# Linear attention into a Swish feed-forward: attention of batch 1 in fewer bursts, another order of loads, later relus

## The chip, the cores and the metric

The kernel runs on one core of a Trainium2 chip. The metric is the device time of one execution in microseconds (us). The core's engines each have a queue of their own and work in the order in which the program issues to them: TensorE (PE; PEld is its load of weights), VectorE (DVE), ScalarE (ACT), GpSimd (POOL) and SyncE (SP), which issues most DMAs.

## The reference, cut to what matters

```python
# q, k, v: (8, 8, 576, 64): batch, head, position, width
phi(x) = concat(relu(x) * cos, relu(x) * sin)     # cos, sin depend on the position
kv  = einsum('bhsf,bhsd->bhfd', phi(k), v);  z = sum_s phi(k)
x   = (phi(q) @ kv) / (phi(q) @ z + 1e-6)         # per batch and head
x   = x.transpose(0, 2, 1, 3).reshape(4608, 512)
h   = x @ w_in                                    # 512 -> 2048
out = (h * sigmoid(beta * h)) @ w_out             # 2048 -> 512
```

## The kernel before, in words

The 4608 tokens are worked through in nine chunks of 512 (eight blocks of 64 tokens). A batch has nine blocks, so chunk 0 holds blocks 0 to 7 of batch 0, chunk 1 block 8 of batch 0 and blocks 0 to 6 of batch 1, chunk 2 blocks 7 and 8 of batch 1 and six of batch 2, and so on. The program is a hand-written order (`manual_schedule`): each engine's queue holds its instructions in the order of the code, and the framework adds the waits that the data need.

**Attention of a batch.** `load_raw` brings queries, keys and values in from SP (L79). `q_relu`, `k_relu` (L192 on ScalarE, L193 on VectorE) and `v_scale` (L217 ScalarE, L219 VectorE) make qb, rk and vb in bf16. The queries are turned, by TensorE (`q_turn_pe`, L235, with copies qt on ScalarE, L240, and products with the tangent, qs, on VectorE, L223) or by a DMA (`q_turn_dma`, L259). `kv_mm` (L276) makes kv of a pair of heads from 36 products on 64x64 tiles, `kv_take` copies it out of PSUM (L286). `num_mm` (L297) makes eight products on 64x64 tiles for one block and one half jp of the heads. `x_rden` and `x_mul` (L308, L312, L319) divide, and xs is turned into xt by TensorE (`x_turn_pe`, L356, copies L361 and L363) or by a DMA from SP (`x_turn_dma`, L367).

**Feed-forward.** `h_mm` (L386) multiplies xt by w_in, for four slices mi of which the first two need the half jp 0 of the heads and the others jp 1; `h_act` (L394) is the Swish on ScalarE. In chunk 0 the second product is plain (`o_mm`, L544, copy L550). For chunk 1 (`o_fast`, L563) and the later ones it is done with sums of blocks (S1 to S4 from the Swish's results, T1 to T4 from w_out, L406 and L876 to L879 on VectorE), seven products "1" to "7" for each pair of token groups; the copies "c1", "cu", "c5", "c4" (L602, L604, L603, L582) and the sums "a2", "a3", "a7" (L606, L607, L608) move partial results between them.

**Chunk 0** has 32 slots. Slots 0 to 15 are the sixteen groups of `h_mm` and `h_act`, slots 16 to 31 the second product, four matmuls of 128x512 for each group and weight slice; slot 24 + i needs slice 8 + i of w_out, which `cast_out` (L121 ScalarE, L123 VectorE) scales into bf16. The table `early` hangs other work behind a slot. Before the change it holds: slot 4, the two `num_mm` of block 8 of batch 0 and `rest()` (casts of w_in, loads of w_out and of batch 1, block 8's `x_mul` and its turn by DMA, casts of w_out, values, keys and queries of batch 1); slot 15, parts of values and keys on ScalarE; slot 22, both `kv_mm` of batch 1; slot 23, `second()`, the turn of its queries; slots 25 and 26, seven blocks of `num_mm` for each half; slots 28 and 29, the turns of xs. At slot 24 the loads of batch 2 are issued.

**Chunk 1** has sixteen slots of `h_group`. Behind slot 0 come blocks 7 and 8 of batch 1 (`num_rest`) and the queries of batch 2, at slots 2 to 5 its values and keys, at slot 6 the sums T, at slot 10 `kv_all(2)` and the tangent. Behind the slots ScalarE makes the relus of batch 3's queries, and only then do the products "1" and their copies "c1" follow.

PSUM has eight banks; the banks that a product takes are named in the code (block 8 took banks 2 and 3, each half of sevens 4 and 5 or 6 and 7, the rest 2 and 3).

Of the kernel before, what the change touches and what calls it, by code (L numbers as in the profile page):

```python
# [22 lines left out]
def kernel(  # L23
# [52 lines left out]
    def load_raw(b, name, j0=0, j1=4):  # L76
        js = slice(j0, j1)
        src = {"q": q, "k": k, "v": v}[name][b]
        nc.sync.dma_start(  # L79
            out=raw_tile(b, name)[:, js].rearrange("q j n d -> q j (n d)"),  # L80
            in_=src.rearrange("(j g) (p n) d -> (g p) j (n d)", g=2, n=NQ)[:, js, :])
# [46 lines left out]
    load_raw(0, "q", 0, 2)  # L128
    load_raw(0, "q", 2, 4)
    beta16 = const.tile([JT, P], FP32, name="beta16")  # L130
    nc.scalar.dma_start(out=beta16, in_=moe_beta.rearrange("(j p) -> j p", p=P))
    load_raw(0, "v", 0, 2)
    load_raw(0, "k", 0, 2)
# [115 lines left out]
    def qs_of(b):  # L249
        return wx["q"] if b > 3 and b % 2 == 0 else qs_first  # L250
# [30 lines left out]
    def kv_take(jps, bank, eng="dve"):  # L281
# [5 lines left out]
        else:  # L287
            nc.vector.tensor_copy(o, a)

    def num_mm(b, n, jp, bank, slot):  # L290

        for cs in range(2):
            for jj in range(2):
                rows = slice(jj * HP, (jj + 1) * HP)
                for g in range(2):
                    cols = slice(g * HP, (g + 1) * HP)
                    nc.tensor.matmul(  # L297
                        ps[cols, bank + jj, slot * E : (slot + 1) * E],
                        lhsT=(qts[b % 2], qs_of(b))[cs][rows, jp, n, cols],
                        rhs=kv[rows, g, jp, cs, :],  # L300
                        start=(cs == 0), stop=(cs == 1))

    def x_rden(bank, slot, n0, n1, jps):

        w, m = len(jps), n1 - n0
        nv = ps[:, bank : bank + 2, slot * E : (slot + w * m) * E].rearrange("q j (i s e) -> q j i s e", s=w, e=E)
        den = small.tile([P, 2, m, w], FP32, name="den", tag=f"den{m}{w}")
        nc.vector.tensor_tensor(  # L308
            den, nv[:, :, :, :, D],
            eps9[:, n0:n1].unsqueeze(1).unsqueeze(3).to_broadcast([P, 2, m, w]), op=ALU.add)  # L310
        rden = small.tile([P, 2, m, w], FP32, name="rden", tag=f"rden{m}{w}")
        nc.vector.reciprocal(rden, den)  # L312
        return nv, rden, n0, jps

    def x_mul(got, n0, n1):
        nv, rden, first, jps = got
        a, z, w = n0 - first, n1 - first, len(jps)
        o = xs[:, n0:n1, jps[0] : jps[-1] + 1].rearrange("q n s (j d) -> q j n s d", j=2)
        nc.vector.tensor_tensor(  # L319
            o.rearrange("q j n s d -> q j (n s) d"),  # L320
            nv[:, :, a:z, :, 0:D].rearrange("q j n s d -> q j (n s) d"),
            rden[:, :, a:z].rearrange("q j n s -> q j (n s)").unsqueeze(3).to_broadcast([P, 2, (z - a) * w, D]),
            op=ALU.mult)
# [432 lines left out]
    def cast_halves(i, fs=(0, 256)):  # L756
        for f in fs:
            for gj in GJ:
                cast_win(i, gj, "pool" if i > 1 and gj == GJ[3] else "dve", f, f + 256)
# [2 lines left out]

    def rest():

        cast_halves(2)
        cast_halves(3)
        x_mul(x_rden(2, 0, 8, NQ, (0, 1)), 8, NQ)
        load_w("out", 0)
        load_w("out", 1)
        load_raw(1, "v")  # L770
        load_raw(1, "k")
        load_raw(1, "q")
        load_w("out", 2, 2)
        load_w("out", 3, 2)
        x_turn_dma(0, 8, 9)
        for j in range(8):
            cast_out(j)
        v_scale(1, 0)
        v_scale(1, 1, n0=8)
        k_relu(1, 0, 2)  # L780
        q_relu(1, 0)
        q_relu(1, 1, n1=5)

# [2 lines left out]
        for n in range(7):  # L786
            num_mm(1, n, jp, bank, n)

    takes = []

    def second():

        takes.append(q_turn_pe(1, 0, 4, hold=True))
        takes.append(q_turn_pe(1, 1, 6, hold=True))
        cast_out(8)
        takes[0]("act", 0)
        takes[0]("dve", 1)
        cast_out(9, "a")
        takes[0]("dve", 0)
        takes[0]("act", 1)  # L800
        cast_out(10)
        for e, i in (("act", 0), ("dve", 1), ("act", 1), ("dve", 0)):
            takes[1](e, i)
        for j in (11, 12, 14, 15):
            cast_out(j, "a")

    early = {
        4: lambda: (num_mm(0, 8, 0, 2, 0), num_mm(0, 8, 1, 2, 1), rest()),
        15: lambda: (v_scale(1, 1, n1=8, eng="act"), k_relu(1, 2, 4, "act")),
        22: lambda: (kv_mm(1, 0, 6), kv_mm(1, 1, 6), kv_take((0, 1), 6, "act"), q_relu(1, 1, "act", 5)),  # L810
        23: second,
        25: lambda: (num_seven(0, 4), x_mul(x_rden(4, 0, 0, 7, (0,)), 0, 7), cast_out(13)),
        26: lambda: (num_seven(1, 6), x_mul(x_rden(6, 0, 0, 7, (1,)), 0, 7)),
        28: lambda: x_turn_pe(1, 0, 7, 4, ("act",), (0,)),
        29: lambda: x_turn_pe(1, 0, 7, 5, ("dve",), (1,)),
    }

    def num_rest():
        for n in range(7, NQ):
            for jp in range(2):  # L820
                num_mm(1, n, jp, 2, 2 * (n - 7) + jp)
        x_mul(x_rden(2, 0, 7, NQ, (0, 1)), 7, NQ)
        x_turn_dma(1, 7, NQ)

# [29 lines left out]
    for slot in range(32):  # L854
        if slot < 4:
            if slot == 0:
                for jt in range(2):
                    h_mm(0, jt, (2, 3), slice(0, 4))
            h_mm(0, slot, (2, 3), slice(4 if slot < 2 else 0, 8))
            h_act(0, slot)  # L860
        elif slot < 16:
            h_group(0, slot)
        elif slot < 24:
            o_part(0, slot % 4, (slot - 16) // 4)
        else:
            for tt in range(4):
                o_mm(0, tt, (slot - 16,))
        if slot == 24:
            for name in "qvk":
                load_raw(2, name)  # L870
        if slot in early:
            early[slot]()

# [5 lines left out]
        nc.vector.tensor_tensor(T3, B22, B12, op=z)  # L879

    wx_tiles()
    for slot in range(16):
        h_group(1, slot)
        if slot == 0:
            num_rest()
            att_q(2)
            v_half(2, 0)
        if 2 <= slot < 6:
            v_half(2, 1, slot + 3, slot + 4, "act")
        if slot == 4:  # L890
            k_all(2)
            v_half(2, 1, 0, 5)
        elif slot == 6:
            w_sums()
        elif slot == 10:
            kv_all(2, eng="act")
            for jp in range(2):
                tan_mul(nc.vector, qs_of(2)[:, jp], qts[0][:, jp], 0, NQ)
    q_relu(3, 0, "act")
    q_relu(3, 1, "act")  # L900
    q_turn_dma(3)

    def one_sums(kind):
        for i0 in range(0, JT // 2, 2):
            g_sum(1, i0, i0 + 2, kind)
# [6 lines left out]
    ops(x, "1 c1")  # L912
    one_sums(1)
    ops(y, "1 c1")
    for t, bank in enumerate((4, 6, 0)):
        num_all(2, t, bank)
    one_sums(2)
# [174 lines left out]
```

## Time and profile before

| what | us |
|---|---|
| median of 3 runs (273.54 to 273.8) | 273.59 |
| the profiled execution | 274.44 |
| its span in the profile | 272.7 |
| PE busy in the span | 265.3 |
| DVE busy | 224.0 |
| ACT busy | 188.4 |
| POOL busy | 68.3 |

The span is what the profile covers of the execution; the rest of the execution's time lies around it. A row of a timeline gives start, length, engine, line, operation, what is written from what, shapes and count; in brackets the idle time before it and who ended it. In the chain of work that ended last, each piece is what the next one waited for, or what stood before it on its engine. Where the page says "L386" it means that line of the kernel.

Chunk 0's second product runs from 31.8 to 50.4 us, chunk 1's first product from 50.4 to 65.9, its second to 80.6.

### The profile page before, as it was taken

How to read it: one execution, taken by the hardware profiler on the slowest of the kernel's cores; microseconds unless marked ns; L12 is line 12 of the kernel's file. 1: busy time of each engine (PE TensorE's matmuls, PEld its weight loads, DVE VectorE, ACT ScalarE, POOL GpSimd, SP SyncE). 2: the span in 40 equal slices, each digit the busy share in tenths (PEclk: the TensorE clock that was granted, in tenths of full speed). 3: DMA queues.
4: the chain of work that ended last, by engine and by line, in shares of the span. 5: the costliest groups of instructions: out<-in, count | busy, mean ns of one | idle time of the engine just before them, and what ended most of it. 6: DMA issues, size and time to landing. Idle time of an engine off the chain costs nothing.

```text
span 272.7 us, 8970 instructions
## 1 busy us (share of the span) xinstructions
PE 265.3 (97%) x3712; PEld 206.8 (76%) x3712; DVE 224.0 (82%) x596; ACT 188.4 (69%) x384; POOL 68.3 (25%) x89
## 2 busy tenths in 40 slices
PE   8899999999899999999999999999999999999994
PEld 8554455455784588888888888888888888888883
DVE  5989969499989889789989997899589768757852
ACT  4778777796419656899489966996696179428920
POOL 1444000510078000660085009300840060000001
PEclk9999999999999999999999999999999999999999
DMA  6999999999969999994589439943600570015005
GB/s 237 374 395 383 392 390 319 379 201 336 284 130 311 240 348 226 240 313 103 147 216 370 92 58 223 332 71 62 181 2 2 61 185 1 2 27 130 0 2 155
DMA packets 50681, 54.00 MB, mean 198 GB/s; under 512 B 31232, under 2 KB 31760, under 8 KB 50640
## 3 DMA queue, kind: packets, MB, share of 16 engines
q1 hardware_dynamic: 47504, 45.55, 59.1%
q0 software_dynamic: 2784, 7.61, 9.6%
q8 instruction: 29, 0.48, 0.7%
q10 hardware_dynamic: 352, 0.27, 0.4%
q14 instruction: 12, 0.10, 0.1%
HBM read 36.71 MB, written 9.44 MB: 169 GB/s over the span
## 4 chain that ended last, share of the span: by engine, by line
PE 85%; DVE 9%; DMA 3%; SPq 1%; issue 1%; ACT 1%; DVEq 0%
PE ps L621 32%; PE ps L511 27%; PE ps L386 10%; PE ps L544 5%; PE ps L563 4%; PE ps L297 3%; DMA raw_v<-in_v_dram 3%; PE ps L276 3%; DVE vb L219 1%; DVE xs L319 1%; DVE qs L223 1%; SPq L79 1%; DVE S L406 1%; DVE rk L193 1%; DVE qb L193 0%
## 5 line engine op out<-in xcount | busy, mean ns | idle before, releaser
L537 POOL DMA_DIRECT2D out_dram<-o_sb x58 | 33.9, 591 | 147.3 <-ACT o_sb L658 86.3
L420 ACT ACTIVATE g_t<-ps,beta 128x512 bf16<-128x512 f32 x96 | 60.3, 702 | 1.4 <-PE ps L511 1.3
L621 PEld LDWEIGHTS <-S 128*128 128x128 bf16 x448 | 43.4, 98 | 5.2
L511 PE MATMUL ps<-w_stage 128*128 128x256 bf16 x288 | 46.6, 272 | 0.1
L386 PE MATMUL ps<-xt,win 128*128 128x512 bf16 (+1 forms) x196 | 42.8, 375 | 0.1
L511 PEld LDWEIGHTS <-w_stage 128*128 128x128 bf16 x384 | 37.3, 98 | 5.1 <-issue 0.2
L487 DVE TENSOR_TENSOR ps<-ps,p 128x256 f32<-128x256 f32 x74 | 30.5, 428 | 8.6 <-PE ps L511 3.0
L394 ACT ACTIVATE g_t<-ps,beta 128x512 bf16<-128x512 f32 x48 | 32.3, 688 | 7.2 <-PE ps L386 7.1
L621 PEld LDWEIGHTS <-g_t 128*128 128x128 bf16 x336 | 32.3, 98 | 4.5 <-ACT g_t L420 0.4
L386 PEld LDWEIGHTS <-win 128*128 128x128 bf16 x196 | 18.7, 98 | 21.1 <-issue 0.5
L511 PE MATMUL ps<-xt,win 128*128 128x256 bf16 x192 | 32.9, 273 | 0.0
L511 PEld LDWEIGHTS <-win 128*128 128x128 bf16 x288 | 28.0, 98 | 3.4
L621 PE MATMUL ps<-wout,g_t 128*128 128x256 bf16 x224 | 28.9, 273 | 0.0
L406 DVE TENSOR_TENSOR S<-g_t 128x512 bf16<-128x512 bf16 (+1 forms) x66 | 25.7, 418 | 3.3 <-ACT g_t L420 1.7
L480 ACT COPY ps<-ps 128x256 f32<-128x256 f32 x62 | 22.6, 383 | 7.5 <-PE ps L621 4.0
L217 ACT ACTIVATE vb<-raw_v,sin 128x256 bf16<-128x256 f32 (+1 forms) x58 | 26.0, 503 | 1.5 <-DMA raw_v<-in_v_dram 1.5
L621 PE MATMUL ps<-T,S 128*128 128x256 bf16 x224 | 26.6, 273 | 0.0
L621 PE MATMUL ps<-wout,S 128*128 128x256 bf16 x224 | 26.4, 273 | 0.0
L319 DVE TENSOR_TENSOR xs<-ps,rden 128x768 bf16<-128x768 f32 (+4 forms) x26 | 22.8, 884 | 0.9 <-DVE rden L312 0.2
L223 POOL TENSOR_TENSOR qs<-qt,tanr 128x1152 bf16<-128x1152 bf16 x6 | 14.3, 2387 | 27.4 <-PE ps L563 21.0
L658 ACT COPY o_sb<-ps 128x512 f32<-128x512 f32 x11 | 6.3, 587 | 20.1 <-PE ps L621 20.1
L487 DVE TENSOR_TENSOR ps<-ps,u 128x256 f32<-128x256 f32 x36 | 15.3, 427 | 5.3 <-PE ps L511 3.3
(112 smaller groups left out, 414.7 us busy)
## 6 DMA issues: line engine op xcount, KB each, us to landing
raw_v<-in_v_dram SPq DMA_DIRECT2D x7, 1152.0 KB, 9.7
raw_k<-in_k_dram SPq DMA_DIRECT2D x7, 1152.0 KB, 9.5
raw_q<-in_q_dram SPq DMA_DIRECT2D x7, 1152.0 KB, 7.4
out_dram<-o_sb POOLq DMA_DIRECT2D x58, 128.0 KB, 4.5
w_stage<-in_moe_w_in_dram SPq DMA_DIRECT2D x3, 1024.0 KB, 12.8
w_stage<-in_moe_w_out_dram SPq DMA_DIRECT2D x2, 1024.0 KB, 7.9
w_stage<-in_moe_w_out_dram SPq DMA_DIRECT2D x4, 512.0 KB, 11.9
out_dram<-o_sb SPq DMA_DIRECT2D x10, 128.0 KB, 2.4
```

The source lines that it names most:

```text
L217: got = nc.scalar.activation(o, a, AF.Copy, scale=t[:, n : n + 1])
L223: return eng.tensor_tensor(dst.rearrange("q n (g p) -> q n g p", g=2), src.rearrange("q n (g p) -> q n g p", g=2), tanr[:, n0:n1].unsqueez ...
L319: nc.vector.tensor_tensor(o.rearrange("q j n s d -> q j (n s) d"), nv[:, :, a:z, :, 0:D].rearrange("q j n s d -> q j (n s) d"), rden[:, :, ...
L386: nc.tensor.matmul(ps[:, h_bank(c, jt), i * 64 : (i + w) * 64], lhsT=win[jt // 4][:, mi, (jt % 4) * P : (jt % 4 + 1) * P], rhs=xt[:, i : i ...
L394: return nc.scalar.activation(gs[c, jt // 4][:, jt % 4], ps[:, h_bank(c, jt)], AF.Silu, scale=beta[:, jt : jt + 1])
L406: return nc.vector.tensor_tensor(o, l, r, op=op)
L420: return nc.scalar.activation(gs[c, jt // 4][:, jt % 4], bank, AF.Silu, scale=beta[:, jt : jt + 1])
L480: return nc.scalar.copy(at("a", 0), at("b", 0))
L487: nc.vector.tensor_tensor(dst, at("b", 0), st["p5"], op=ALU.add)
L511: nc.tensor.matmul(dst, lhsT=l[:, g], rhs=r[:, :, g * HP : (g + 1) * HP], start=start and g == 0, stop=g == 1, skip_group_check=True)
L537: (eng or own).dma_start(out=out_v[bb, n][:, m0:m1], in_=o_sb[hf * HP : (hf + 1) * HP, m0:m1])
L621: nc.tensor.matmul(dst, lhsT=l(i), rhs=r[:, i], start=start and i == 0, stop=i == order[-1], skip_group_check=True)
```

## The change

It does the following:

- A small DMA on ScalarE's queue reads eight values from each half of each head of batch 0's v into a tile `touch` that nothing uses. It stands ahead of the load of beta.
- Block 8 of batch 0 moves from slot 4 to slot 27, in front of `kv_mm` of batch 1. As the queries' tile qs holds batch 1 by then, GpSimd copies block 8's part of qs aside at slot 4 (`qs_last`, in the space of S2). Its `x_mul` and its turn by DMA move along, and the loads of batch 2's values and keys are issued behind that turn, the load of its queries ahead of it.
- SP loads batch 1's queries ahead of w_out 2 and its keys behind w_out 2.
- The turn of batch 1's queries moves from slot 23 to slot 22, its keys' relus behind it, and `kv_mm` from slot 22 to slot 27. Both halves of seven blocks come together at slot 28, and the turns of xs at slots 30 and 31. Several `cast_out` change their place or engine.
- In chunk 1 the first half (mi 0 and 1) of the first four groups comes ahead of their second half; `num_rest` moves from slot 0 to slot 10, in front of `kv_all(2)`, and its division behind that.
- The relus of batch 3's queries and their turn by DMA move behind the products "1" and copies "c1" of chunk 1.

```diff
--- before.py
+++ after.py
@@ -128,6 +128,8 @@
     load_raw(0, "q", 0, 2)
     load_raw(0, "q", 2, 4)
     beta16 = const.tile([JT, P], FP32, name="beta16")
+    touch = const.tile([2 * H, 8], FP32, name="touch")
+    nc.scalar.dma_start(out=touch, in_=v[0].rearrange("h (s r) d -> (h s) r d", s=2)[:, 0, 0:8])
     nc.scalar.dma_start(out=beta16, in_=moe_beta.rearrange("(j p) -> j p", p=P))
     load_raw(0, "v", 0, 2)
     load_raw(0, "k", 0, 2)
@@ -287,6 +289,8 @@
         else:
             nc.vector.tensor_copy(o, a)
 
+    qs_last = S2.rearrange("q i t -> q (i t)")[:, 0 : 2 * P].rearrange("q (s c) -> q s c", s=2)
+
     def num_mm(b, n, jp, bank, slot):
 
         for cs in range(2):
@@ -296,7 +300,8 @@
                     cols = slice(g * HP, (g + 1) * HP)
                     nc.tensor.matmul(
                         ps[cols, bank + jj, slot * E : (slot + 1) * E],
-                        lhsT=(qts[b % 2], qs_of(b))[cs][rows, jp, n, cols],
+                        lhsT=(qts[b % 2][rows, jp, n, cols] if cs == 0 else
+                              qs_last[rows, jp, cols] if (b, n) == (0, NQ - 1) else qs_of(b)[rows, jp, n, cols]),
                         rhs=kv[rows, g, jp, cs, :],
                         start=(cs == 0), stop=(cs == 1))
 
@@ -762,22 +767,20 @@
 
     def rest():
 
+        nc.gpsimd.tensor_copy(qs_last, qs_first[:, :, NQ - 1])
         cast_halves(2)
         cast_halves(3)
-        x_mul(x_rden(2, 0, 8, NQ, (0, 1)), 8, NQ)
         load_w("out", 0)
         load_w("out", 1)
         load_raw(1, "v")
-        load_raw(1, "k")
         load_raw(1, "q")
         load_w("out", 2, 2)
+        load_raw(1, "k")
         load_w("out", 3, 2)
-        x_turn_dma(0, 8, 9)
         for j in range(8):
             cast_out(j)
         v_scale(1, 0)
         v_scale(1, 1, n0=8)
-        k_relu(1, 0, 2)
         q_relu(1, 0)
         q_relu(1, 1, n1=5)
 
@@ -786,39 +789,62 @@
         for n in range(7):
             num_mm(1, n, jp, bank, n)
 
-    takes = []
-
-    def second():
-
-        takes.append(q_turn_pe(1, 0, 4, hold=True))
-        takes.append(q_turn_pe(1, 1, 6, hold=True))
-        cast_out(8)
+    def turn():
+
+        takes = [q_turn_pe(1, jp, 4 + 2 * jp, hold=True) for jp in range(2)]
         takes[0]("act", 0)
         takes[0]("dve", 1)
-        cast_out(9, "a")
+        cast_out(8)
         takes[0]("dve", 0)
         takes[0]("act", 1)
+        cast_out(9, "a")
+        takes[1]("act", 0)
+        takes[1]("dve", 1)
         cast_out(10)
-        for e, i in (("act", 0), ("dve", 1), ("act", 1), ("dve", 0)):
-            takes[1](e, i)
-        for j in (11, 12, 14, 15):
+        cast_out(11, "a")
+        takes[1]("act", 1)
+        takes[1]("dve", 0)
+        k_relu(1, 0, 2)
+        k_relu(1, 2, 4, "act")
+        cast_out(12, "a")
+
+    def eighth():
+        load_raw(2, "q")
+        for jp in range(2):
+            num_mm(0, 8, jp, 4, jp)
+        kv_mm(1, 0, 6)
+        kv_mm(1, 1, 6)
+        kv_take((0, 1), 6, "act")
+        cast_out(13)
+        x_mul(x_rden(4, 0, 8, NQ, (0, 1)), 8, NQ)
+        x_turn_dma(0, 8, NQ)
+        load_raw(2, "v")
+        load_raw(2, "k")
+
+    def sevens():
+        for jp in range(2):
+            num_seven(jp, 4 + 2 * jp)
+        for j in (14, 15):
             cast_out(j, "a")
+        for jp in range(2):
+            x_mul(x_rden(4 + 2 * jp, 0, 0, 7, (jp,)), 0, 7)
 
     early = {
-        4: lambda: (num_mm(0, 8, 0, 2, 0), num_mm(0, 8, 1, 2, 1), rest()),
-        15: lambda: (v_scale(1, 1, n1=8, eng="act"), k_relu(1, 2, 4, "act")),
-        22: lambda: (kv_mm(1, 0, 6), kv_mm(1, 1, 6), kv_take((0, 1), 6, "act"), q_relu(1, 1, "act", 5)),
-        23: second,
-        25: lambda: (num_seven(0, 4), x_mul(x_rden(4, 0, 0, 7, (0,)), 0, 7), cast_out(13)),
-        26: lambda: (num_seven(1, 6), x_mul(x_rden(6, 0, 0, 7, (1,)), 0, 7)),
-        28: lambda: x_turn_pe(1, 0, 7, 4, ("act",), (0,)),
-        29: lambda: x_turn_pe(1, 0, 7, 5, ("dve",), (1,)),
+        4: rest,
+        15: lambda: (v_scale(1, 1, n1=8, eng="act"), q_relu(1, 1, "act", 5)),
+        22: turn,
+        27: eighth,
+        28: sevens,
+        30: lambda: x_turn_pe(1, 0, 7, 4, ("act",), (0,)),
+        31: lambda: x_turn_pe(1, 0, 7, 5, ("dve",), (1,)),
     }
 
     def num_rest():
         for n in range(7, NQ):
             for jp in range(2):
                 num_mm(1, n, jp, 2, 2 * (n - 7) + jp)
+
+    def x_rest():
         x_mul(x_rden(2, 0, 7, NQ, (0, 1)), 7, NQ)
         x_turn_dma(1, 7, NQ)
 
@@ -865,9 +891,6 @@
         else:
             for tt in range(4):
                 o_mm(0, tt, (slot - 16,))
-        if slot == 24:
-            for name in "qvk":
-                load_raw(2, name)
         if slot in early:
             early[slot]()
 
@@ -879,10 +902,15 @@
         nc.vector.tensor_tensor(T3, B22, B12, op=z)
 
     wx_tiles()
+    for jt in range(4):
+        h_mm(1, jt, (0, 1))
     for slot in range(16):
-        h_group(1, slot)
+        if slot < 4:
+            h_mm(1, slot, (2, 3))
+            h_act(1, slot)
+        else:
+            h_group(1, slot)
         if slot == 0:
-            num_rest()
             att_q(2)
             v_half(2, 0)
         if 2 <= slot < 6:
@@ -893,13 +921,11 @@
         elif slot == 6:
             w_sums()
         elif slot == 10:
+            num_rest()
             kv_all(2, eng="act")
+            x_rest()
             for jp in range(2):
                 tan_mul(nc.vector, qs_of(2)[:, jp], qts[0][:, jp], 0, NQ)
-    q_relu(3, 0, "act")
-    q_relu(3, 1, "act")
-    q_turn_dma(3)
-
     def one_sums(kind):
         for i0 in range(0, JT // 2, 2):
             g_sum(1, i0, i0 + 2, kind)
@@ -912,6 +938,9 @@
     ops(x, "1 c1")
     one_sums(1)
     ops(y, "1 c1")
+    q_relu(3, 0, "act")
+    q_relu(3, 1, "act")
+    q_turn_dma(3)
     for t, bank in enumerate((4, 6, 0)):
         num_all(2, t, bank)
     one_sums(2)
```

## The prediction

> **What bounds the kernel now.** I read the page first: TensorE is busy for 97% of the span at a full granted clock, and the chain that ended last is 85% TensorE.
>
> ```profile
> PE 265.3 (97%) x3712; PEld 206.8 (76%) x3712; DVE 224.0 (82%) x596; ACT 188.4 (69%) x384; POOL 68.3 (25%) x89
> PEclk9999999999999999999999999999999999999999
> PE 85%; DVE 9%; DMA 3%; SPq 1%; issue 1%; ACT 1%; DVEq 0%
> ```
>
> So a change can pay in three ways: shorten the start before TensorE's unbroken stretch, take a stall out of it, or take TensorE time out of it. The chain in order of time shows all three (start, length, what):
>
> ```profile
> 3.16 9.06 DMA raw_v<-in_v_dram
> 12.22 0.02 issue
> 12.25 0.92 DVE vb L209
> ...
> 22.07 0.25 PE ps L297 x16
> ...
> 37.97 1.15 PE ps L276 x72
> 39.12 0.97 PE ps L544 x4
> ...
> 42.98 0.58 PE ps L297 x56
> 43.56 0.97 PE ps L544 x4
> 44.53 0.18 PE ps L297 x5
> 44.71 0.61 PE ps L297 x40
> ...
> 51.39 0.44 PE ps L297 x32
> ...
> 66.66 2.02 DVE S L406 x6
> 68.69 1.15 ACT qb L192
> 69.83 0.27 ACT p L602
> 70.10 0.04 issue
> 70.15 10.64 PE ps L563 x96
> ```
>
> To 12.25 the values' DMA decides; then VectorE to 18.65; from there TensorE, broken only near 70. There L563 (the second products of chunk 1's output) stands still, by the list of waits:
>
> ```profile
> PE ps L563 <- ACT p L602: 1.0, 1, 1.0
> ```
>
> ScalarE's timeline shows why: the copy p stands behind two relus that wait for batch 3's queries.
>
> ```profile
> 67.62 2.22 ACT L192 ACTIVATE qb<-raw_q 128x1152 bf16<-128x1152 f32 x2 [0.82 <-DMA raw_q<-in_q_dram]
> 69.74 0.63 ACT L602 COPY p<-ps 128x256 f32<-128x256 f32 x2
> ```
>
> **Bursts.** Attention products run on 64x64 tiles. From the rows, 16, 32 and 56 of them take 0.25, 0.44 and 0.58 us: 0.008 us each and about 0.12 us on top. Leaving costs again: four L544 products take 0.97 us behind a burst and 0.86 elsewhere. A burst thus costs some 0.22 us beyond its work. Now there are six (block 8, kv of batch 1, two sevens, the rest, kv of batch 2); after the change three. Saved: 3 x 0.22 = 0.66 us. The second seven took 0.79 us instead of 0.58; whether that goes too is open, so I take 0.70 in all, with 0.4 (leaving alone saved, with a little of the entry) and 0.87 as ends.
>
> **The stall.** The relus and their transpose move behind both L602 copies, so the first copy can run when its product is done: 0.96 us of idle TensorE goes. What is late next? The product "6" needs S2 (VectorE). By VectorE's timeline S2's last piece ends at 69.34 and "6" started at 70.15. VectorE is full from 51.92 to 77.9, so I follow it through.
>
> **VectorE in chunk 1, after.** The rest of batch 1 (0.16 + 0.20 + 0.69 us with gaps, 1.05) moves from 51.92 behind the weight sums at slot 10, its instructions unchanged. Batch 2's relus can then start when the jp-1 copy of xt ends, near 50.8, and end at 52.2. The values of batch 2 landed at 40.83 + 11.5 = 52.3, the keys at 41.43 + 13.8 = 55.2; I expect the same (below). Sums: cosine values 52.35 + 2.4 = 54.7; keys' relu 55.3 to 56.6; sine 57.9; four weight sums (4.8) 62.7; rest 63.75; tangent (2.55) 66.3; S1 and S2 (1.34 each) 69.0. That is only 0.36 us ahead of before, with TensorE 1.3 us ahead. Before the y adds at the end of the chunk VectorE stood idle 0.26 us (78.20, by TensorE) and its add of the seventh product ended at 78.95 against TensorE's use at 79.75: 1.06 us of room, with 0.36 makes 1.4. So the stall goes almost wholly; I charge 0.10 us for S2 pieces and for bank 4, which the first x product of batch 2 holds to about 70.3. ScalarE's relus end near 69.9, the copies cu behind them near 70.3 and 71, needed at 72. The transpose of batch 3's queries then leaves at 69.9 on SP, as now (69.86), so what queues behind it on SP (three transposes of xs, the load of batch 4's queries) and GpSimd's tangent at 76.5 keep their times.
>
> **Slots 22 to 31.** Query transposes move to slot 22. The DMA list gives the landings: w_out 0 at 27.4, 1 at 30.1, values 33.1, keys 36.1, queries 39.2, w_out 2 at 40.5 and 41.9, w_out 3 at 43.3 and 44.5. Queries in the keys' place land at 36.1, w_out 2 at 37.5 and 38.9, keys at 41.8, w_out 3 unchanged. Query relus end near 37.3, TensorE comes at 37.9. VectorE in slots 22 to 27: four tangents (0.67 or 0.8), two casts (0.4), keys' relu (0.76), end 43.0. ScalarE: four copies (0.6), two casts (0.65), keys' relu (1.15), end 43.4. TensorE opens the joint burst (num 8, then kv) at 43.45 and wants ScalarE's half of the keys 0.7 us later. The kv copy ends 45.4 under slot 28's 0.87 us, so the sevens start at about 45.65. x_mul of jp 1 ends 49.25, wanted 49.7. These covers are 0.1 to 0.7 us thick: cost nothing, but each late microsecond is a microsecond of the path.
>
> Block 8's turn moves from 34.3 to its x_mul in slot 27, 44.8 on SP. Ahead of it in the DMA queue is now the load of batch 2's queries (waits only for relus done at 37.3, lands 47.5); behind it the values and keys of batch 2, which SP can issue only after it. Chunk 1's first product needs it at 50.1. Rows for this transpose, issue to landing: 2.8 us (73.4, 74.8, 77.7), 6.7 (53.08, beside output stores), 10.5 (34.3, behind 10.2 us of loads, so it landed 0.3 us after them). Here 2.7 us of loads are ahead and no store: I take 47.9, nearest to the last row counted from the end of its backlog. SP's time for it was 1.2 to 2.7 us; 1.2 where the queue wasn't full, so values leave at 46.1 and the queue does not run dry.
>
> [...]
>
> The joined halves of chunk 1's first four groups leave ScalarE (0.60 us a group) 1 us behind TensorE; the bank wanted again at 55.3 is free at 54.2: nothing. GpSimd's copy of qs, bounded by 0.29 us (128x128 select) and 2.4 (128x1152 product), lies in GpSimd's 3.2 us wait before the third weight's cast: nothing.
>
> **The start.** The early read is a DMA issue on ScalarE's queue ahead of beta's. Beta's took 0.45 us, the first table load stood right behind it at 1.29, so cos9 comes about 0.49 us later; VectorE's tangent, TensorE's broadcast and the query relus hang on it. VectorE runs full from 4.36 to 12.06, then waits 0.19 for values. The delay left at 12.25: 0.49 less 0.19, + 0.30 us. Could the read itself help? DMA traffic dipped to about 300 GB/s when the values began (5.3 to 6.5 us), some 0.4 us lost; but values landing earlier than 12.2 meet a VectorE that is late. Ends: - 0.19 (issue hidden, values early) and + 0.49. I take + 0.30.
>
> **Sum.** + 0.30 - 0.70 - 0.96 + 0.10 = - 1.26 us, from the span of 272.7: 271.4. The profiled execution took 274.44, 1.74 more than its span; the median of the runs shown, 273.59, is 0.85 below it. Forecast on the median: 273.59 - 1.26 = **272.3**, its own range 271.6 to 273.0.
>
> **Rivals.** A, *VectorE becomes the bound* of chunk 1. If SP takes 2.7 us for the turn, the values leave at 47.6, the queue runs dry for a microsecond, keys land at 56.4 and each VectorE term shifts by 1.1: the y add ends near 79.4, TensorE gains 0.2 there. For it: VectorE's unbroken row from 51.92 to 77.9. Against: the 1.2 us rows. 273.4, chance 0.14.
>
> B, *the turn is late*, the slower side. Place: chunk 1's first product. It decides from a landing at 50.1, and cancels the gain from 51.4. With 6.7 us it lands at 51.5 (273.7), with 10.5 at 55.3 (277.5); in the middle 275.6. For it: two of the three rows of this mixture of loads and turn. Against: the backlog that made them. Chance 0.14.
>
> C, *the keys are late*: if they come only behind w_out 3, at 44.5, ScalarE's relu ends at 45.7 and kv waits 1.6 us: 273.9. Against: the landings follow the order of issue, 1.4 us for each half of w_out. Chance 0.10.
>
> The forecast keeps 0.62. About 0.2% (0.55 us) is what a measurement of this kernel can tell from no change. Faster 0.62; within it A and half of C, 0.19; slower B and half of C, 0.19. The range takes the forecast's ends, A and C and B's near end: 271.6 to 274.2.
>
> **What would show it.** Right: three bursts (88, 112 and 104 products) in place of six up to 62 us; no L563 wait on L602; TensorE's first 128x128 stretch starting 0.3 us later than 18.65; xt's turn landing before 50. Wrong: TensorE idle before L276 near 44 (C), before L386 near 50 (B), before L297 or L563 from 67 to 70 on VectorE's qs or S (A).

## The result, and the profile after

The changed kernel takes **276.56 us** (median of 6, 275.05 to 278.01) beside 273.58 for the kernel before on the same chip (median of 6, 273.37 to 273.93): ratio 1.0112, 95% interval 1.0073 to 1.0151. It is 3 us slower where 1.3 us faster was forecast, and its runs lie 3 us apart where those of before lie 0.6 apart; the two longest (278.01 and 277.91) had a mean granted TensorE clock of 0.990 and 0.992, the other four 0.998 or more. The profiled execution took 276.95, with a span of 275.2.

The head of the page looks as before: TensorE works as long (265.2 us against 265.3), at a mean granted clock of 1.000 over the span (0.998 before). Only the shares of the chain differ: "issue", time in which an engine waited for nothing that the profile shows, has 2%, and VectorE 2% instead of 9.

```profile
PE 265.2 (96%) x3712; PEld 207.0 (75%) x3712; DVE 224.0 (81%) x596; ACT 187.9 (68%) x384; POOL 67.7 (25%) x90
PE 93%; DVE 2%; issue 2%; ACT 1%; ACTq 0%; DVEq 0%
```

The chain of the changed kernel in order of time (start, length, what) holds that 2% in two pieces:

```profile
43.41 1.02 PE ps L278 x72
44.43 0.97 PE ps L549 x4
45.40 0.56 PE ps L301 x53
45.96 1.83 issue
47.79 0.70 PE ps L301 x51
...
69.03 1.09 PE ps L301 x111
70.12 1.54 issue
71.67 0.44 PE ps L301 x29
72.11 10.59 PE ps L568 x96
```

Lines have moved by 2 to 5: L301 is the `num_mm` product (L297 before), L278 the `kv_mm` product, L549, L391 and L568 the plain output product, the first product and chunk 1's output product. The planned order is there, close to its forecast times: block 8 and kv in one burst from 43.16 (forecast 43.45), the sevens from 45.40 (45.65), the output products (L568) right behind batch 2's 144 products with no wait on a copy. But TensorE stands still for 1.83 us **in the middle of the sevens**, and for 1.54 us in the middle of batch 2's 144 products. The view by windows (length, then busy time of PE, PEld, DVE, ACT and POOL, granted clock, DMA share) shows that in the first of them the clock is whole, and nobody works much:

```profile
44.00:46.00 2.00, 1.96 (x89) 1.09 (x77) 0.60 (x2) 1.65 (x4) 0.00 (x0) 1.00 0.89 325
46.00:47.80 1.80, 0.01 (x4) 0.01 (x4) 0.00 (x0) 0.30 (x1) 0.00 (x0) 1.00 0.29 74
```

### The profile page after: what moved, and what is told of

Read it like the earlier page. It is cut to its first block, busy times and chain, and to the rows that moved or that the text cites. A ratio compares the mean times of both kernels' runs of the same rounds, so it can differ in the third digit from the quotient of the medians.

```text
span 275.2 us, 8972 instructions
## 1 busy us (share of the span) xinstructions
PE 265.2 (96%) x3712; PEld 207.0 (75%) x3712; DVE 224.0 (81%) x596; ACT 187.9 (68%) x384; POOL 67.7 (25%) x90
## 4 chain that ended last, share of the span: by engine, by line
PE 93%; DVE 2%; issue 2%; ACT 1%; ACTq 0%; DVEq 0%
PE ps L626 32%; PE ps L516 27%; PE ps L391 15%; PE ps L549 5%; PE ps L568 4%; PE ps L301 4%; PE ps L278 3%; PE ps L237 1%; PE ps L684 1%; DVE xs L324 1%; DVE win L115 1%; PE ps L680 1%; ACT L158 0%; PE ps L694 0%; PE ps L361 0%
## 5 line engine op out<-in xcount | busy, mean ns | idle before, releaser
L542 POOL DMA_DIRECT2D out_dram<-o_sb x58 | 33.0, 576 | 150.2 <-ACT o_sb L663 86.5
L391 PE MATMUL ps<-xt,win 128*128 128x512 bf16 (+1 forms) x196 | 42.6, 375 | 0.3 <-DVE win L115 0.2
L391 PEld LDWEIGHTS <-win 128*128 128x128 bf16 x196 | 18.9, 98 | 21.6 <-POOL win L113 0.6
L221 DVE TENSOR_SCALAR vb<-raw_v,cos 128x256 bf16<-128x256 f32 x63 | 19.3, 357 | 1.2 <-DMA raw_v<-in_v_dram 1.2
```

The lines of the kernel that those rows point to most:

```text
L221: got = nc.vector.tensor_scalar(o, a, scalar1=t[:, n : n + 1], scalar2=None, op0=ALU.mult)
L391: nc.tensor.matmul(ps[:, h_bank(c, jt), i * 64 : (i + w) * 64], lhsT=win[jt // 4][:, mi, (jt % 4) * P : (jt % 4 + 1) * P], rhs=xt[:, i : i ...
L542: (eng or own).dma_start(out=out_v[bb, n][:, m0:m1], in_=o_sb[hf * HP : (hf + 1) * HP, m0:m1])
```

## Two theories

The products behind each stop read tiles that the products ahead of it were reading already, and the profile shows nothing that they waited for. What else does TensorE need? The page's third part has a queue that I had passed over:

```profile
q8 instruction: 29, 0.48, 0.7%
```

29 packets of 16 KB, which the page counts, like the loads of data, as a share of the core's 16 DMA engines (0.7%). TensorE has 3712 weight loads and 3712 products; a load with its product is a pair below, and 29 times 128 pairs is 3712. (The count alone proves little: kernels below with 3741 pairs have 29 packets too.) **Theory 1**, to be tested: TensorE's instructions arrive in blocks of 128 pairs, through the same DMA engines as the loads of data, and TensorE stops when the next block is not there. In each of the twelve traces of this case that hold every record, the block k (counted from 0, as the queue shows them) that came soonest started near product 128k + 74 of the program (128k + 73 to 128k + 80, products counted from 0), so I take that product as the moment of asking; this is an inference. Both stops came at one place in the count: before product 603 = 3 x 128 + 219, and before product 987 = 6 x 128 + 219. So between asking and need lie 145 products. If they are 128x512 products of 0.216 us each (28 took 6.04 us before), that is 31 us; if most of them are 64x64 products of 0.008 us each, as in the prediction's rows, it may be 3 us. The DMA records give (us; "asked" is product 128k + 74, "needed" product 128k + 219):

| kernel, block | asked | started | landed | needed | stop |
|---|---|---|---|---|---|
| before (second profile, below), 3 | 37.96 | 41.60 | 42.69 | 44.40 | none |
| changed, 3 | 43.09 | 45.43 | 46.50 | 45.96 | 1.83 |
| before (second profile), 6 | 62.56 | 65.89 | 66.90 | 68.40 | none |
| changed, 6 | 64.10 | 69.06 | 70.17 | 70.12 | 1.54 |

TensorE went on 1.3 and 1.5 us after the landing. The joint bursts had put 88 products of 64x64, four slow ones and 53 of 64x64 into one window: 2.9 us between asking and need, where it was 6.4 in the kernel before.

**Theory 2**: a long run of 64x64 products stops by itself, by some limit of its own; the place then belongs to the burst and not to the count.

## The experiments

### 17 more products ahead of the bursts

```diff
-            o_part(0, slot % 4, (slot - 16) // 4)
+            o_part(0, slot % 4, (slot - 16) // 4, 2 if 17 <= slot < 22 else 1)
```

> The changed kernel with five of the 512-column products of chunk 0's output (slots 17 to 21) each split into halves along the columns: the same numbers, 17 more instructions on TensorE ahead of the bursts, next to no work added. Theory 1 (TensorE runs out of loaded instructions: a block of 128 weight loads and products is asked for when the block before the last is used up, lands late while loads fill the DMA queues, and TensorE stops at product 128k + 219): the block whose late landing stopped the sevens at 45.96 is asked for 17 products sooner, while slow products run, near 40 instead of 43.1 us, so the stop of 1.83 us goes; the one of 1.54 us near 70 moves 17 products ahead in the program, is asked for near 61.6 instead of 64.1, and goes or shrinks. 272.4 to 274.0 us. Theory 2 (a long run of 64x64 products stops by itself, whatever its place in the program): both stops stay behind the same products of their bursts; 276.5 us as the changed kernel.

Measured 276.34 us (274.42 to 277.72), ratio to before 1.0097 (1.0064 to 1.0131). The chain:

```profile
45.51 0.41 PE ps L301 x36
45.92 0.85 issue
46.77 0.84 PE ps L301 x74
```

The stop came behind the 36th product of the sevens instead of the 53rd: 17 earlier in the burst, at the same 603 in the count. It did not vanish: the block was asked for 3.9 us sooner, near 39.2, but started only 1.0 us sooner, at 44.40. The stop near 70 us is gone (landed 67.0, needed 68.9). The total did not follow the forecast of 272.4 to 274.0: near 155 us a stop of 0.61 us appeared (block 16 landed at 154.09, TensorE went on at 155.49), and chunk 2 waited 0.70 us for xt at 80.2. The profile puts the 0.61 down to a wait for ScalarE, but its distance from the packet is that of the other stops, and so is its place: before product 2265 = 16 x 128 + 217, where four kernels below stop too. So 219 holds for blocks 3 and 6 and shifts a little along the program. So the place in the count is as theory 1 has it, and my price for the cure was wrong: a shift moves every later block too.

### 12 products fewer at the start

```diff
-    warm_pe(58, 48)
+    warm_pe(46, 60)
```

> The changed kernel with the 58 warm-up products of 48 columns at the start replaced by 46 of 60 columns: about the same time of warming, 12 instructions fewer on TensorE ahead of everything. Theory 1 (TensorE runs out of loaded instructions at product 128k + 219): the stop in the sevens comes 12 products later in the program, behind about the 65th product of the 112 instead of the 53rd, and the one in the third batch's attention behind about the 123rd instead of the 111th; lengths between 1 and 2.5 us, since less slow work lies ahead of each; 275 to 278 us. Theory 2 (a long run of 64x64 products stops by itself): both stops stay behind the 53rd and the 111th product; 276.5 us.

Measured **283.71 us** (282.78 to 283.93), 1.0358 (1.0332 to 1.0383), far above the 275 to 278 that I expected. The place moved as theory 1 has it, and there were more stops than I had counted on:

```profile
14.24 0.66 PE ps L278 x26
14.90 2.42 issue
...
48.88 0.65 PE ps L301 x62
49.53 0.45 issue
...
71.11 1.19 PE ps L301 x114
72.31 3.00 issue
```

By the weight loads, which are all recorded, the stop in the sevens came behind their 65th product instead of the 53rd, again before product 603, and the one in batch 2's 144 products behind the 127th instead of the 115th, before 987 (a row of the chain counts only the pieces on it, hence x62 and x114). Both are twelve later in their bursts. Block 0, asked for at 6.7, started at 15.02 beside the first loads; that is the new stop at 14.9, in `kv_mm` of batch 0, before product 222. A fourth (1.47 us) stands at 187.6. Twelve products that the result does not need, left out at the start, cost 7 us.

The stops themselves are some 4 us of that: they add up to 7.34 us in this profile and to 3.37 in the changed kernel's. The windows around the longest show the rest:

```profile
72.30:75.30 3.00, 0.01 (x1) 0.00 (x0) 2.93 (x9) 1.33 (x2) 0.00 (x0) 1.00 1.85 281
75.30:76.60 1.30, 1.30 (x27) 1.15 (x28) 1.23 (x5) 0.00 (x0) 0.00 (x0) 1.00 0.28 28
76.60:80.00 3.40, 3.40 (x19) 2.42 (x17) 1.91 (x5) 0.74 (x2) 0.00 (x0) 0.50 1.38 214
```

1.3 us behind the stop the granted clock falls to 0.50 for 3.4 us, and the products of chunk 1's output start 0.21 us apart instead of 0.11. The same stands at 18.6 us, 1.3 us behind the stop of 2.42; the mean granted clock of this execution is 0.987. From 3.4 us at 0.50 I estimate a cost of up to 1.7 us for each such stretch. The changed kernel's profile has none behind its two stops (1.00 from 47.8 to 52 and from 71.7 to 85 us); why some stops bring it isn't shown.

### Without the loads of batch 3's keys and values

```diff
+        if b == 3 and name in "kv":
+            return
```

> The changed kernel without the loads of batch 3's keys and values: batch 3 is computed with batch 2's keys and values instead, and 4.7 MB of loads are left out near 57 to 70 us. TensorE's program is the same, instruction for instruction. Theory 1 (TensorE's instructions come through the same DMA engines and land late behind loads): the block that was asked for at 64.1 us starts within 1.5 us instead of 4.96, and the stop of 1.54 us near 70 goes; the stop of 1.83 us in the sevens, whose block was asked for at 43.1 beside loads that are still there, stays; 274.5 to 275.5 us. Theory 2 (a long run of 64x64 products stops by itself): both stops stay; 276.5 us. If the stop near 70 stays at its length with its block landed early, theory 1 falls.

(The loads left out are two of 1152 KB, 2.4 MB; the 4.7 in the expectation is a slip.) Measured 275.04 us (274.53 to 277.21), 1.0065 (1.0038 to 1.0092). The stop near 70 is gone, with the same program on TensorE: block 6 started 2.6 us after product 842 instead of 5.0 (I had expected 1.5 at most), and had landed 1.5 us before it was needed. The stop in the sevens is there with its 1.83 us; in this profile, of an execution of 277.14 us with a mean granted clock of 0.994, the clock falls to 0.50 for 3.4 us right behind it. So the loads beside it were about half of this block's delay, and enough to make the stop.

### The later relus alone, in the kernel before

```diff
-    q_relu(3, 0, "act")
-    q_relu(3, 1, "act")
-    q_turn_dma(3)
     ops(x, "1 c1")
     one_sums(1)
     ops(y, "1 c1")
+    q_relu(3, 0, "act")
+    q_relu(3, 1, "act")
+    q_turn_dma(3)
```

> The kernel before with one part of the change alone: the relus of batch 3's queries and their transpose behind the two copies of chunk 1's c product. Theory 1 and theory 2 alike: the bursts are those of before, so no stop is added, and the wait of 0.96 us of the output products on ScalarE's copy goes: 272.6 to 272.9 us. Under theory 1 there is one proviso: the products near 70 us run 0.9 us sooner, while the block of instructions that they need was asked for at 62.9 and started at 65.4; before, it was there 2 us ahead, so the cover holds. If the time is unchanged, TensorE stops elsewhere near 70 us and the wait was not worth what I took it for.

Measured 273.74 us (273.13 to 274.70, 12 runs), beside 273.60 for before: 1.0001 (0.9984 to 1.0017). No gain, though its own profile has no wait near 70 and took 273.16. So how common is that wait?

### The kernel before, profiled a second time

> The kernel before, not changed, for a second profile. The run with the later relus alone gained 1.0 us between 61.6 and 97.6 us of its profile, yet its median is that of the kernel before. If the wait of 0.96 us of the output products on ScalarE's copy is in this profile too, the later relus lose their gain elsewhere; if it is not, or much smaller, the profiled execution of before (0.85 us over its median) was one of the few with that wait, and the gain that I priced from it was mostly not there to take. Time: 273.1 to 274.9 us either way.

It took 273.16 us, and the wait is not there. The chain, and ScalarE's timeline behind it:

```profile
67.49 1.36 PE ps L297 x136
...
68.89 10.64 PE ps L563 x96
```

```profile
66.37 2.21 ACT L192 ACTIVATE qb<-raw_q 128x1152 bf16<-128x1152 f32 x2
```

Batch 3's queries had landed in time, the relus ran at 66.37 instead of 67.62, the two copies behind them were done at 69.11, and TensorE went from one row into the next with 0.04 us between. The one profile that my forecast rests on was an execution 0.85 us over the median, and it held this wait of 0.96 us. By the medians, the later relus take away something that most executions do not have.

### The sevens as two bursts again

```diff
-        for jp in range(2):
-            num_seven(jp, 4 + 2 * jp)
+        num_seven(0, 4)
...
+        29: second_seven,
```

> The changed kernel with the two sevens as bursts of their own again, one in slot 28 and one in slot 29, with four of the output's products (0.9 us) between them. Theory 1 (TensorE stops at product 603 of its program until the late block of instructions has landed): the stop stays where it is in the count, and the four slow products take the place of some of it: it shrinks from 1.83 to about 0.9 us, and the total stays within 0.3 us of the changed kernel's 276.3 to 276.6, because TensorE goes on at the same moment. Theory 2 (the merged burst itself is too long): with bursts of 56 as in the kernel before the stop of 1.83 us goes, 1.6 to 1.8 us faster than the changed kernel.

Measured 275.83 us (275.69 to 275.96), 1.0083 (1.0067 to 1.0098).

```profile
45.31 0.56 PE ps L301 x52
45.87 1.78 issue
47.64 0.22 PE ps L301 x3
```

Theory 2 falls: a burst of 56 stops as well, before product 603. My number for theory 1 was wrong too: the stop comes within the first seven, ahead of the four slow products (47.87 to 48.84), which so cannot take its place. The total is 0.7 us under the changed kernel's; in the profile the second stop has 0.47 us instead of 1.54, as block 6 came 0.9 us sooner.

### Without the early read

```diff
-    touch = const.tile([2 * H, 8], FP32, name="touch")
-    nc.scalar.dma_start(out=touch, in_=v[0]...)
```

> The changed kernel without the early read of the values. My prediction put + 0.30 us on this read, by its issue on ScalarE's queue ahead of beta's. By that, TensorE's first stretch of 128x128 products starts 0.1 to 0.3 us earlier than in the changed kernel, and the total falls by as much, under the changed kernel's own spread: 275.5 to 276.5 us. Rival: the read brings the values in earlier; without it the stretch starts later than in the changed kernel. The two stops of TensorE stay, since its program is the same.

Measured 276.06 us (274.95 to 276.88), 1.0088 (1.0059 to 1.0118), which the spread of the changed kernel covers. TensorE's first stretch of 128x128 products in chunk 0 starts at 18.98 here, at 18.80 in the changed kernel (18.65 and 18.39 in the two profiles of before). With the read, VectorE's first half of the values comes 0.46 us later (9.62 against 9.16), as I had priced it, but the second half can start at 11.95 instead of 12.57. So the issue costs what I said and is paid back before 18 us; with one profile of each I can't tell a gain from nothing.

### 29 more products

> The changed kernel with the 512-column products of slots 17 to 24 of chunk 0's output split into halves along the columns: 29 more instructions ahead of the bursts where the run with 17 had a stop of 0.85 us left in the sevens. Theory 1: the block is asked for near 37.8 us instead of 39.9; if it starts at the same distance (4.5 us) it is there in time and the stop goes, if it waits for the same loads to end (start at 44.4) some 0.4 us of it stays; the second stop stays gone. 273.0 to 274.5 us, and less spread than the changed kernel's 3 us. Theory 2 (a long burst stops by itself): 276.3 us, both stops in place.

The same edit for slots 17 to 24. Measured 277.26 us (276.78 to 277.97), 1.0137 (1.0116 to 1.0159), over 2.7 us above the forecast. Both stops are gone: the sevens ran in one piece, and blocks 3 and 6 landed over 2.4 us before their need. TensorE was 0.2 us ahead of the kernel before (second profile) at the end of batch 2's kv, 61.07 against 61.26, and lost it all behind: from there to the second group of chunk 2's output products it took 36.9 us where before takes 35.05. And block 16 brought a stop of 1.49 us at 153.5, before product 2265. In the chain, what sets the pace of chunk 1 is now this:

```profile
46.76 10.25 DMA raw_k<-in_k_dram
...
57.03 1.36 DVE rk L195
...
68.13 2.69 DVE S L411 x8
...
72.20 8.97 PE ps L568 x80
```

Batch 2's keys land at 57.0, VectorE had waited for them since 54.9. That is what rival A of my prediction forecast, VectorE as the bound of chunk 1, hidden in the changed kernel by the stops. Its reason was another, though: SP took 1.28 us for block 8's turn here and not 2.7, the values left at 46.06 as in my forecast, and the keys were late all the same.

### The same without the load of batch 2's keys, and with VectorE in another order

```diff
+        if (b, name) == (2, "k"):
+            return
```

> The kernel with 29 more instructions (in its profile the sevens ran without a stop, and the output products of chunk 1 waited for VectorE instead) without the load of batch 2's keys: batch 2 is computed with batch 1's keys, which are there. In the run with 29 the keys came at 57.0 us and VectorE's chain from them to S set TensorE's pace up to 72.2 us; from 61.07 to 97.95 us it took 36.9 us where the kernel before takes 35.05 when nothing waits. If the late keys are the cause (my rival A), VectorE starts on them near 54.5, the waits of TensorE on qs and S vanish, and that stretch takes 35.0 to 35.4 us; the stop near 153.5 us, which belongs to the count of instructions, can stay; total 274.0 to 275.8 us. If VectorE's own work is what is too long, the stretch stays near 36.5 us and the total near 277.

Measured 275.31 us (273.85 to 278.29), 1.0045 (1.0017 to 1.0072). The stretch took 34.96 us, no wait on VectorE, the sevens in one piece (`45.31 1.20`), and the stop before product 2265 stayed with 1.19 us. At the end of the stretch this run is 0.5 us ahead of the kernel before. So the load of the keys decides: because the keys come late, or because of its place in the queue? This edit puts 2.5 us of other work of VectorE into its wait:

```diff
-            k_all(2)
             v_half(2, 1, 0, 5)
+            nc.vector.tensor_tensor(T1, B12, B11, op=ALU.subtract)
+            k_all(2)
```

> The kernel with 29 more instructions, and VectorE's work of chunk 1 in another order: the sine values of batch 2 (5 instructions, 1.3 us) and the first of the four weight sums (1.2 us) ahead of the keys' relu, in the 2.1 us in which VectorE waited for the keys. Nothing is left out. If the late keys are what made TensorE wait in the run with 29, S ends near 68.7 us instead of 70.8, the waits on qs and S go, and the stretch from the first products behind batch 2's kv to the first output group of chunk 2 takes 35.0 to 35.4 us (36.9 in the run with 29, 35.0 without the keys' load). The stop near 152 us is one of the count and can stay with 0 to 1.5 us: 272.3 to 274.3 us. If the stretch stays over 36 us, VectorE was not late by the keys but by its work.

> The same with 25 more instructions instead of 29 (slot 24's four products whole again): the version that should be the fastest by theory 1. The block whose late landing gives the stop near 152 us is needed four products (0.44 us) later, so that stop shrinks by about 0.4 us; the block of the sevens is asked for 0.9 us later and, with 1.1 us to spare in the last two profiles, is still there in time. 271.9 to 273.9 us. If a stop comes back in the sevens, the time between asking and landing has jumped, as it did in the run with 17.

Measured 277.49 us (275.16 to 279.04), 1.0128 (1.0092 to 1.0164), and 278.22 us (276.55 to 279.00), 1.0155 (1.0131 to 1.0179). Both miss. VectorE was ready at 63.2, and then waited for another transfer, the turn of batch 2's queries:

```profile
52.00 13.00 DMA qt<-qb
...
65.03 2.63 DVE qs L225 x2
```

The stretch took 36.8 and 37.0 us. So the late keys alone are not it, and VectorE's work is not either: behind them the next transfer is late too. The turn left SP at 52.0 and landed at 65.0; in the second profile of before it left at 54.1 and landed at 62.1. The values and keys of batch 2 leave SP at 46.1 and 46.8 instead of 40.8 and 41.4, behind block 8's turn, and the turn of batch 2's queries lands behind them. No run put them ahead of that turn again, so this order as the cause is argued and not shown. And block 16 came later still (5.5 and 5.6 us behind product 2122, stops of 1.62 and 1.77 us): the four products that I gave it back were less than what its start varies by.

### What made the second block late

In the kernel before with the later relus, only the rest of batch 1's products, division and turn move from slot 0 to slot 10, one burst of 104 with kv:

```diff
-            num_rest()
             att_q(2)
...
+            num_rest()
             kv_all(2, eng="act")
+            x_rest()
```

> The kernel before with two parts of the change that by the runs so far should do no harm: the later relus, and the rest of batch 1's products moved from slot 0 to slot 10 of chunk 1, ahead of the kv products of batch 2, so that two bursts become one of 104 products. Saved: one burst's 0.22 us, and the 0.96 us wait in those executions that have it. Theory 1: the count at which TensorE can run out of instructions (731) lies in slow products, as it did, so no stop is added; 273.0 to 273.5 us, the 0.22 us seen in the profile between the first product of chunk 1 and the end of batch 2's kv. Theory 2 (a long burst stops by itself): a stop of about 1.5 us in the burst of 104, 274.5 to 275 us. If it is over 273.8 without a stop, VectorE's later rest of batch 1 is what is late.

Measured 274.47 us (273.97 to 276.86, 12 runs), 1.0041 (1.0020 to 1.0062).

```profile
67.35 1.09 PE ps L297 x109
68.44 1.43 issue
69.88 0.44 PE ps L297 x26
```

The burst of 104 ran through (59.78 to 61.18), but the stop at product 987 is here, in a burst that the edit does not touch. I had looked only at the count 731. Two runs tell why block 6 is late.

> The kernel before with the later relus, and with the division and the transposing DMA of the rest of batch 1 moved to slot 10 of chunk 1, while its products stay a burst of their own in slot 0. In the run with the joined burst of 104 products a stop of 1.43 us came behind the 111th product of batch 2's attention at 68.4 us: its block of instructions started at 67.46 instead of 65.9, asked for at the same 62.4. Two reasons are open. (a) The transposing DMA at 64.3 us is beside it in the queues and delays it: then the block starts as late here (4.5 to 5 us after 62.4), and the stop of about 1.4 us is here too; 274.0 to 274.8 us. (b) The joined products move the block before (asked for at 55.7 instead of 51.2, started at 61.4 instead of 54.2), and this one is delayed behind it: then the block before starts near 54 here, this one 2.4 to 3.3 us after 62.4, and there is no stop; 273.0 to 273.8 us.

> The kernel before with the later relus and the joined burst of 104 products, and the transposing DMA of the rest of batch 1 issued only behind batch 2's attention products and the sums next to them, near 72 us (chunk 2 needs it from 80.7). (a) If that DMA is what delays the block of instructions, the block asked for at 62.4 starts by 65.7, the stop at the 111th product goes, and the kernel gains the burst's 0.22 us: 272.9 to 273.5 us, as fast as the kernel before or a little faster. (b) If the joined burst itself moved the requests together, the block starts near 67.4 and the stop of 1.4 us stays: 274.0 to 274.6 us.

The division and the turn moved to slot 10, the products left at slot 0: 273.92 us (273.37 to 278.78), 1.0021 (0.9998 to 1.0045), block 5 starts at 56.4, block 6 2.2 us after it is asked for, no stop. The products and the division moved, the turn put off to 73.6: 274.66 us (274.54 to 275.23), 1.0046 (1.0032 to 1.0060), with the stop, 1.35 us. So it is the joined products: they bring product 714, at which block 5 is asked for, from 51.2 to 55.7 us, block 5 starts at 61.4 to 61.6 instead of 54.2, and block 6 starts 6.1 us behind it. That spacing is the same in five kernels with the joined burst (61.40 to 67.46, 61.58 to 67.69, 62.95 to 69.06, 62.06 to 68.20, 62.39 to 68.47): the two of this section, the changed kernel, the one with the sevens split and the one without the early read. It is not a constant: without batch 3's loads it is 3.8, with 12 products fewer 8.2, and over 10 where more products ahead have block 5 asked for by 53 us. What sets it to 6.1 us stays open.

No kernel here beats the one before.

## Why the prediction was wrong

The sum failed at a term that it did not have: the stops that theory 1 puts down to **the supply of TensorE's own instructions**. I priced each edit by TensorE's work and by waits for data, wrote "These covers are 0.1 to 0.7 us thick: cost nothing", and gave the joined bursts no cost of their own. The runs showed two stops in place of that nothing: 1.83 us in the joined sevens and 1.54 us in batch 2's products. Against the second profile of before, which has no wait near 70, the changed kernel loses 0.42 us to the start of chunk 0's products (18.78 to 19.20), then 1.1 us to the end of batch 2's kv (1.83 for the stop, 0.7 won back), then 1.6 us in chunk 1 (1.54 for the stop), and 0.6 us in the long rest, whose cause was not looked for: 3.8 us in the two profiles, 273.16 and 276.95.

- *Bursts, - 0.70.* Right in itself: six bursts took 4.97 us with their exits in the first profile of before and 4.75 in the second, three take 4.21 without the stops, 0.76 or 0.54 less. But joining them is what brought the stops, the first by block 8, kv and the sevens, the second by the rest and kv of batch 2.
- *"The second seven took 0.79 us instead of 0.58; whether that goes too is open."* It was the sign that I should have followed: its 0.2 us of delay lies right before product 603 (44.51 to 44.71), and the second profile of before has none there. By the place it is block 3, just late already; but TensorE went on 1.80 us after that block's landing, later than behind any stop, so this isn't shown.
- *The stall, - 0.96.* It left as forecast, but it was no property of the kernel: one of two profiles of before has it, and taking it away alone changed the median by nothing (1.0001). The profiled execution's 0.85 us over the median was a sign of it; I moved my sum to the median without asking which wait the 0.85 was.
- *VectorE in chunk 1, + 0.10.* Wrong in its inputs: "the keys at 55.2; I expect the same"; they came at 56.9 (and at 56.35 already in the second profile of before). Rival A had about this time (56.4), by SP's 2.7 us for the turn, and gave it 0.14; SP took 2.25 us here and 1.28 in the run with 29 more products, with the keys at 57.0 in both. In the changed kernel the stops hide it; with the stops out of the way, that stretch takes 1.8 us more.
- *The start, + 0.30.* The issue on ScalarE's queue cost 0.46 us as worked out, and the values' second half came 0.6 us sooner. Undecided, and small.
- *Block 8's turn, the keys, x_mul.* The covers held: the turn took SP 2.25 us and was in time, keys' relu on ScalarE ran from 42.1 to 43.3, before kv. Rivals B and C did not happen.

Most blocks brought no stop: 29 of them in each of sixteen traces gave nineteen stops of 0.4 us or more. In the twelve traces that hold every record the soonest block started at product 128k + 73, 146 pairs ahead of product 128k + 219; where those 146 were short, a stop took up to 3.0 us.

## What to carry to other kernels

Look at the queue of instructions in the profile of every kernel whose bound engine has many short instructions, and work out for each block how long the products between asking and need (145 here) last. Beside the loads, blocks 2 to 7 took 2.1 to 6.6 us to start in the first profile of before and in the changed kernel's, with a median of 1.1 to land, and TensorE went on 1.3 to 1.6 us behind the landing where it had stopped. Windows of 2.9 and 6.0 us brought the changed kernel's two stops, windows of 6.4 and 5.8 us in the kernel before brought none: near 6 us both happened. Long products between the short ones, as in the kernel before, were worth more here than the 0.2 us that each joined burst saves. And before a wait is priced from one profile, see whether that execution lies at the median; if not, take a second profile.

## What the runs showed of the hardware

- In twelve kernels TensorE made nineteen stops of 0.4 us or more that theory 1 would explain; each time it went on 1.27 to 1.60 us after the end of a 16 KB packet. That it waited for instructions in that packet is inferred from the places and times.
- In the sixteen traces a block's packet took 0.9 to 1.4 us in nine of ten cases and 3.8 at most. In the changed kernel it started, in the median, 1.2 us after product 128k + 74 behind 200 us, where few loads run, and 5.2 us after it for blocks 2 to 7.
- Behind three stops, of 1.83 us without batch 3's loads and of 2.42 and 3.00 us with 12 products fewer, the granted clock fell to 0.50 for 3.4 us, 0 to 1.3 us after TensorE went on; the mean granted clock of these two executions is 0.994 and 0.987. In the other ten kernels with stops it is 0.996 to 1.000, where one such stretch alone would bring it to 0.994 or less: none of their stops brought a whole one.
- With 17 products more ahead of the bursts the stop in the sevens came behind their 36th product, with 12 fewer behind their 65th, instead of the 53rd: each time before product 603. The 12 fewer cost some 7 us against the changed kernel.
